# The last expert's second layer by token halves, with one of its two scatters moved ahead of a branch

## The chip, the cores and the metric

The kernel runs on one core of one Trainium2 chip. The metric is the device time of one execution in microseconds (us). Before the change the median of three executions was 429.29 us (428.25 to 430.55). One further execution was recorded by the hardware profiler and took 431.34 us.

Five engines run side by side, each with its own instruction sequence: TensorE (PE in the profile, with its weight loads as PEld), VectorE (DVE), ScalarE (ACT), GpSimd (POOL) and SyncE (SP). They meet only through semaphores. A suffix q (POOLq, ACTq) marks the sequencer of an engine: the part that reads instructions, waits for semaphores, loads registers and takes branches.

## The reference, cut to what matters

```python
attn_out = _attn_ref(q, k, v, s)                 # 2 x 8 heads, 576 rows, 64 wide
x = attn_out.transpose(0, 2, 1, 3).reshape(1152, 512)
x = _moe_ref(x, ...)                             # 8 experts, capacity 288
# second mixture: each token goes to one of 8 experts, 144 tokens each
for e in range(8):
    mask = assigned == e
    h = np.maximum(x[mask] @ w1[e], 0.0)         # 144 x 512 @ 512 x 1024
    out[mask] = h @ w2[e]                        # 144 x 1024 @ 1024 x 512
```

The change is in the last lines: the product `h @ w2[e]` of the eighth expert of the second mixture, and the way its 144 rows get to `out`.

## The kernel before, in words

The program is one long sequence: attention, routing, eight experts of the first mixture, routing, eight experts of the second mixture. Only the end matters here.

**One expert of the second mixture** (`moe2`, L2105) holds its 144 tokens as columns. The first layer (`layer1`, L992, matmuls on L1004 to L1006) makes `h`, 1024 by 144, in two 16-bit parts: a high part written by ACT (L1012) and a low part written by DVE (L1013). The second layer (`second2`, L2051) multiplies by `w2`. For the last expert `w2` too is held in two 16-bit parts; the low part is written by DVE on L164. So an output block of 128 features is 8 slices times 3 terms, 24 matmuls of 144 columns (L2059), in the order (high w, high h), (low w, high h), (high w, low h) for slice 0, then slice 1, and so on. Four blocks of features make 96 matmuls. Two blocks share a tile of PSUM, the accumulator memory, and ACT copies each finished pair to `y` (L2065).

**The rows go out** in two halves of 72 tokens (`turned2`, L2071; `out2`, L2084). PE turns a half of `y` by four transposes (L2075), an engine multiplies it with the gate weights (ACT on L2078, for the very last half DVE on L2080), and POOL issues an indirect DMA that scatters 72 rows of 512 numbers to `out` (L2085). For the experts before the last this happens during the next expert's work. For the last expert the two halves lie in the tiles named `XA` and `iotat`.

**The branch.** The routing checks itself (`checks`, L2021). All engines load a flag, `badi`, and skip a long repair block if it is zero (L2190, L2191):

```python
bv = nc.values_load(badi[0:1, 0:1], min_val=0, max_val=4 * E)
with tc.If(bv > 0):
    ...
last_rows()
```

The two last scatters are issued by `last_rows` (L2099), that is behind the branch, because the repair block writes the same rows. Their row numbers, `tokl` (L2045), point out of range when the check has failed, so that nothing is written then. A path that skips the block brings the semaphore counts to what the block would have made them (POOL: the instruction on L2191 called INC_SWDGE_SEM in the trace and ISA in the order of instructions).

**What sets the order.** Every engine works strictly through its own list, in the order in which the Python code emits instructions; a string of letters (`LAST`, L2165) places background steps at numbered points of an expert.

Of the kernel before, what the change touches and what calls it, by code (L numbers as in the profile page):

```python
# [9 lines left out]
F32 = mybir.dt.float32  # L10
# [3 lines left out]
AF = mybir.ActivationFunctionType  # L14
OP = mybir.AluOpType
# [6 lines left out]
def tile_attention_moe_moe(ctx: ExitStack, tc: tile.TileContext, q, k, v, s, wg1, w1a, w2a, capacity,  # L22
                           wg2, w1b, w2b, out, dbg=None):
    nc = tc.nc
    B, H, S, D = q.shape
    NTOK, DM = out.shape
    E = wg1.shape[1]
    FF = w1a.shape[2]
    CAP = int(capacity)
    P = 128  # L30
# [8 lines left out]
    CAP2 = NTOK // E  # L39
# [6 lines left out]
    C0, C1 = max(CAPS), min(CAPS) // 16 * 16  # L46
# [61 lines left out]
    given = set()  # L108
# [719 lines left out]
    for m in range(-7, NH + 3):  # L828
# [47 lines left out]
        for name in names:  # L876
            if m == NH - 1 and name == "X1":
                continue
            if name in tasks:
                tasks[name]()  # L880
                step0(m, name)
                if (m, name) in SCATTER0:
                    n = SCATTER0.index((m, name))
# [90 lines left out]
    def split_ws(i):  # L974
        def of(k, part):
            while (i + k, part) in split_queue and i >= 2 * E:
                pop_hi()
            while (i + k, part) in late:
                pop_lo()
            hi, lo = WS[i + k]  # L980
            return part_of((hi, lo), k, part)
        return of
# [9 lines left out]
    def layer1(p, ws, xt, N, after, tick=none, halved=8):  # L992

        h = p.get("h", hp).tile([P, 8, C0], F32, name="h")
        hh, hl = (x[:, :, :N] for x in h[:, :halved].rearrange("p c n -> p (c n)").bitcast(F16).rearrange(
            "p (k c n) -> k p c n", k=2, c=halved)) if halved else (None, None)
        h = h[:, :, :N]
        for fp in range(4):
            ph = p["ph"].tile([P, 2, N], F32)
            wh, wl = ws(0, fp)  # L1000
            for g in range(2):
                fs = slice(g * P, (g + 1) * P)
                for c in range(4):
                    nc.tensor.matmul(ph[:, g], wh[:, c, fs], xt[:, c], start=c == 0, stop=False)  # L1004
                    nc.tensor.matmul(ph[:, g], wh[:, c, fs], xt[:, 4 + c], start=False, stop=False)  # L1005
                    nc.tensor.matmul(ph[:, g], wl[:, c, fs], xt[:, c], start=False, stop=c == 3)  # L1006
                if g == 0:
                    tick(3 * fp)
            tick(3 * fp + 1)
            r = slice(2 * fp, 2 * fp + 2)  # L1010
            if 2 * fp < halved:
                nc.scalar.activation(hh[:, r], ph, AF.Relu)  # L1012
                nc.vector.scalar_tensor_tensor(hl[:, r], ph, 0.0, hh[:, r], op0=OP.max, op1=OP.subtract)  # L1013
            else:
                nc.scalar.activation(h[:, r], ph, AF.Relu)
            after(fp)
            tick(3 * fp + 2)
        return hh, hl, h
# [19 lines left out]
    def rows_of_w2(i, hs, halved):  # L1038

        w = loaded[i].rearrange("p (c f) -> p c f", c=8)  # L1040
        hh, hl, h = hs
        terms = [(w, h, f) for f in range(halved, 8)]
        if halved:
            while any(x[0] == i for x in split_queue):
                pop_hi()
            while any(x[0] == i for x in late):
                pop_lo()
            wh, wl = (x.rearrange("p (c f) -> p c f", f=DM) for x in WS[i])
            terms = [(a, b, f) for f in range(halved) for a, b in ((wh, hh), (wl, hh), (wh, hl))] + terms
        return terms  # L1050
# [65 lines left out]
    mo1, mo2 = {}, {}  # L1116
# [87 lines left out]
    S2 = CAP2 // 2  # L1204
# [200 lines left out]
    pend = None  # L1405
    for e in range(E):
# [14 lines left out]
        halved = 8 if e in HELD else 4 if e else 0  # L1421
        hs = layer1(mo1, split_ws(2 * e), XT1.pop((e, 0)), CAPS[e], after1, halved=halved)
# [7 lines left out]
        else:  # L1430
            ys = second1(mo1, 2 * e + 1, hs, halved, CAPS[e], after2)
            pend = (e, ys)
# [124 lines left out]
    gates = []  # L1557
# [157 lines left out]
    def pop_hi():  # L1715
        if split_queue:
            i, part = split_queue.pop(0)
            split_hi(i, part)
            late.append((i, part))

    def pop_lo():
        if late:
            split_lo(*late.pop(0))
# [94 lines left out]
    for t in range(NTT - 1):  # L1818
        nc.tensor.matmul(pp[:, t + 1:], ones, left[:, t:t + 1].to_broadcast([P, NTT - 1 - t]),
                         start=False, stop=t == NTT - 2, skip_group_check=True)  # L1820
# [17 lines left out]
    for t in range(NTT):  # L1838
        cm = gp.tile([P, CT, P], F16, name="g").rearrange("p t q -> p (t q)").bitcast(BF16)
        nc.vector.tensor_scalar(cm, iotac, pos[:, t:t + 1], None, op0=OP.is_equal)  # L1840
        for c in range(CT):
            nc.tensor.matmul(pL[:, c], cm[:, c * P:(c + 1) * P], S3[:, :, t], start=t == 0 and c == 0,
                             stop=t == NTT - 1 and c == CT - 1, skip_group_check=True)
# [10 lines left out]
    A = rp.tile([P, CN, E], F32, name="A")  # L1854
# [193 lines left out]
    tokl = rp.tile([S2, 2], I32, name="tokl")  # L2048
    pb2 = Banks("D1")

    def second2(i, hs, halved, tick):  # L2051
        terms = rows_of_w2(i, hs, halved)
        y = mo2["y"].tile([P, 4, C0], F32, name="y")[:, :, :CAP2]
        for dp in range(2):
            py = mo2["py"].tile([P, 2, CAP2], F32)
            for g in range(2):
                d = slice((2 * dp + g) * P, (2 * dp + g + 1) * P)
                for k, (a, b, f) in enumerate(terms):
                    nc.tensor.matmul(py[:, g], a[:, f, d], b[:, f], start=k == 0, stop=k == len(terms) - 1)  # L2059
                    if k == len(terms) - 5:  # L2060
                        tick(12 + 5 * dp + 2 * g)
                if g == 0:
                    tick(13 + 5 * dp)
            tick(15 + 5 * dp)
            nc.scalar.activation(y[:, 2 * dp:2 * dp + 2], py, AF.Copy)  # L2065
            if dp:
                given.add(i // 2)
            tick(16 + 5 * dp)
        return y

    def turned2(e, y, g2, q_, xo, banks, engine):  # L2071
        pb = banks.tile([P, 512], F32)[:S2].rearrange("p (c d) -> p c d", c=4)
        sl = slice(q_ * S2, (q_ + 1) * S2)
        for c in range(4):
            nc.tensor.transpose(pb[:, c], y[:, c, sl], identf)  # L2075
        pb = pb.rearrange("p c d -> p (c d)")
        if engine == "A":
            nc.scalar.activation(xo, pb, AF.Copy, scale=g2[:, q_:q_ + 1])  # L2078
        else:
            nc.vector.tensor_scalar(xo, pb, g2[:, q_:q_ + 1], None, op0=OP.mult)  # L2080

    scattered = []

    def out2(rows, xo):  # L2084
        i = nc.gpsimd.indirect_dma_start(  # L2085
            out=out[:, :], out_offset=bass.IndirectOffsetOnAxis(ap=rows, axis=0),
            in_=xo, in_offset=None, bounds_check=NTOK - 1, oob_is_err=False)
        for o in scattered:
            tc.declare_no_dep(i.ins, o.ins, reason="distinct rows")
        scattered.append(i)  # L2090

    def back2(e, y, g2, q_):
        xo = mo2["o"].tile([SL, DM + E + 1], F32, name="x2f")[:S2, :DM]
        turned2(e, y, g2, q_, xo, pb2, "A")
        out2(tok[:, e, q_:q_ + 1], xo)

    xl = [x[:S2].bitcast(F32)[:, :DM] for x in (XA.rearrange("p c n -> p (c n)"), iotat)]

    def last_rows():  # L2099

        scattered.clear()
        for h in range(2):
            out2(tokl[:, h:h + 1], xl[h])

    def moe2(script, first=False):  # L2105
        pend = None
        given.difference_update(range(E, 2 * E))
        for e in range(E):
            i0 = 2 * E + 2 * e

            def tick(k, e=e):
                if first and (e, k) == (E - 1, 0):
                    nc.gpsimd.drain()
                for c in script(e, k):
                    if c == "h":
                        pop_hi()
                    elif c == "l":
                        pop_lo()
                    elif c in "01":
                        if pend is not None:  # L2120
                            back2(*pend, int(c))
                            if first and (e, c) == (E - 2, "0"):
                                nc.gpsimd.drain()
                    elif c == "w":
                        next(work, None)
                    elif e + 1 < E:
                        XT1[e + 1] = spread(xg[e + 1], XT1.get(e + 1), "st".index(c))
                        if c == "t":
                            del xg[e + 1]
                    load_next()  # L2130
                    gather_next()

            halved = HALVED2[e]
            hs = layer1(mo2, split_ws(i0), XT1.pop(e), CAP2, none, tick, halved)
            pend = (e, second2(i0 + 1, hs, halved, tick), gates[0])
            gates.pop(0)
        pbl = Banks("D1 A1")
        for q_ in range(2):
            if first:
                turned2(*pend, q_, xl[q_], pbl, "AD"[q_])  # L2140
            else:
                back2(*pend, q_)

    def steps():
        yield from phases()
# [16 lines left out]
    THEN = "w h l h l0 w w . . . w 1l h wl h l wh l s tl wh l"  # L2162
    FLOAT = "w . . . 0 w w . . . w 1l h wl h l wh l s tl wh l"
    MORE = "w h l h l0 wh wl . . . w 1l h wl h l wh l s tl wh l"
    LAST = "w h l h l0 wh wl h l . w 1 . w . . w . . . w ."  # L2165
    AGAIN = [x.split() for x in [{0: FLOAT, 4: THEN, 6: MORE}[n] for n in HALVED2[:-1]] + [LAST]]
    SCRIPTS = [FIRST.split(), SECOND.split()] + AGAIN[2:]
    next(work)
# [80 lines left out]
```

## Time and profile before

| | |
|---|---|
| median of three executions | 429.29 us |
| profiled execution | 431.34 us |
| its span in the trace | 429.5 us |
| rest around the span | 1.84 us |
| PE busy | 394.1 us (92%) |
| DVE, ACT, POOL busy | 334.3, 258.5, 192.4 us |
| span from the last expert's transposes (421.64) to the end | 7.9 us |

The span is counted from the first instruction to the last. Busy times include the pipeline's depth, and those of different engines overlap. A line of the timeline gives start, duration, engine, source line, operation and tiles; x19 means that 19 instructions were merged into the line. A sequencer's row gives how often an instruction ran, its shortest, median and longest duration in ns, and the first and last start.

### The profile page before, as it was taken

To read this page: it belongs to the slowest core of one execution; us is meant where nothing else is said; L and a number is where in the kernel's file an instruction comes from. 1 tells how busy PE (TensorE), PEld (TensorE's weight loads), DVE (VectorE), ACT (ScalarE), POOL (GpSimd) and SP (SyncE) were. 2 spreads that over 40 slices of the span, in tenths; PEclk is the share of its full clock that TensorE was granted. 3 is DMA by queue.
4 is the path that set the end of the run, shared out by engine and by line. 5 is a ranking of instruction groups with operands and counts; after the bars stand their busy time and mean duration, and the time that the engine had idled before them with its cause. 6 is when DMAs were issued, how large, how long until landed. Compare 5 with 4: busy or idle time off the path is not lost.

```text
span 429.5 us, 14026 instructions
## 1 busy us (share of the span) xinstructions
PE 394.1 (92%) x5408; PEld 364.3 (85%) x5408; DVE 334.3 (78%) x969; ACT 258.5 (60%) x466; POOL 192.4 (45%) x310
## 2 busy tenths in 40 slices
PE   1669999998889999999999999988999999989993
PEld 1448888887768899999999998946999999989993
DVE  7879999989684566777688796688587887988860
ACT  4448888886564165564665681716365766867761
POOL 4378788885781433052141364641243333333021
PEclk9988999999957999999999999966999999999998
DMA  7798898985847669999999976159989999998811
GB/s 138 170 223 191 198 206 217 218 207 168 303 166 186 238 188 363 301 287 365 347 334 332 344 133 111 28 150 319 339 269 346 334 311 323 281 331 289 260 44 34
DMA packets 91327, 103.04 MB, mean 240 GB/s; under 512 B 56136, under 2 KB 59208, under 8 KB 91251
## 3 DMA queue, kind: packets, MB, share of 16 engines
q1 hardware_dynamic: 85859, 91.85, 74.0%
q0 software_dynamic: 4192, 9.91, 7.6%
q8 instruction: 44, 0.72, 0.7%
q10 hardware_dynamic: 1200, 0.30, 0.3%
q14 instruction: 32, 0.26, 0.2%
HBM read 81.42 MB, written 14.59 MB: 224 GB/s over the span
## 4 chain that ended last, share of the span: by engine, by line
PE 66%; DVE 15%; DMA 11%; issue 4%; ACT 2%; SPq 1%; POOL 1%; POOLq 0%; DVEq 0%; ACTq 0%
PE C L1061 12%; DMA xg<-x2d,tok 6%; PE C L2059 4%; PE A L1004 4%; PE A L1006 4%; PE A L1005 4%; PE pog L559 4%; DVE wl L164 4%; PE pT L452 4%; PE pM L476 2%; PE A L2059 2%; DMA cb<-cumd 2%; PE pE L528 2%; PE pE L529 2%; PE D L2059 2%
## 5 line engine op out<-in xcount | busy, mean ns | idle before, releaser
L164 DVE TENSOR_TENSOR wl<-wf,wh 128x1024 bf16<-128x1024 f32 x64 | 78.1, 1242 | 21.6 <-ACT wh L160 21.0
L160 ACT ACTIVATE wh<-wf 128x1024 f16<-128x1024 f32 x64 | 65.6, 1049 | 15.1 <-DMA wf<-in_moe_w_dram 15.1
L1004 PE MATMUL A<-xt,wh 128*128 128x144 f16 (+4 forms) x288 | 59.6, 232 | 0.0
L1006 PE MATMUL A<-xt,wl 128*128 128x144 f16 (+4 forms) x288 | 59.6, 231 | 0.0
L1005 PE MATMUL A<-xt,wh 128*128 128x144 f16 (+4 forms) x288 | 59.6, 231 | 0.0
L1061 PE MATMUL C<-h,wf 128*128 128x160 f32 (+7 forms) x544 | 58.5, 269 | 0.0
L1006 PEld LDWEIGHTS <-wl 128*128 128x128 bf16 x512 | 50.4, 99 | 1.8 <-issue 1.8
L1176 POOL DMA_INDIRECT x2d<-xo,tix x14 | 24.3, 1732 | 61.2 <-DVE l L1193 23.7
L1004 PEld LDWEIGHTS <-wh 128*128 128x128 f16 x512 | 50.5, 99 | 0.7 <-issue 0.5
L1005 PEld LDWEIGHTS <-wh 128*128 128x128 f16 x512 | 50.4, 99 | 0.7 <-issue 0.3
L164 DVE TENSOR_TENSOR wf<-wf,wf 128x1024 bf16<-128x1024 f32 x33 | 39.5, 1219 | 3.4 <-ACT wf L160 3.4
L414 POOL TENSOR_TENSOR pl<-pf,ph 128x512 f16<-128x512 f32 x30 | 35.7, 1202 | 10.0 <-DVE ph L403 7.9
L536 ACT ACTIVATE pf<-pE,XB 128x512 f32<-128x512 f32 (+4 forms) x80 | 36.5, 509 | 4.9 <-PE pE L531 4.5
L1551 POOL DMA_INDIRECT xg<-x2d,tok x16 | 20.0, 1251 | 42.3 <-PE A L2059 10.2
L1061 PEld LDWEIGHTS C<-h,wf 128*128 128x128 f32 x256 | 36.2, 190 | 0.1
L488 DVE CUSTOM_DVE_ANT_0 junk<-pM,cb 128x128 f16<-128x128 f32 (+4 forms) x80 | 32.0, 430 | 4.4 <-PE pM L478 2.7
L160 ACT ACTIVATE wf<-wf 128x1024 f16<-128x1024 f32 x33 | 34.4, 1051 | 0.0
L476 PE MATMUL pM<-al,ar 128*128 128x128 f16 (+2 forms) x96 | 26.9, 320 | 7.2 <-DVE rm L488 7.0
L2085 POOL DMA_INDIRECT out_dram<-x2f,tok x14 | 17.1, 1220 | 35.1 <-ACT h L1012 17.7
L2059 PE MATMUL C<-h,wf 128*128 128x144 f16 (+1 forms) x324 | 31.9, 251 | 0.4 <-DVE wf L164 0.3
L559 PE MATMUL pog<-vf,pf 128*128 128x65 f32 x180 | 30.7, 296 | 0.0
L2059 PEld LDWEIGHTS <-wf 128*128 128x128 f16 (+1 forms) x408 | 26.2, 98 | 1.1 <-issue 0.5
(455 smaller groups left out, 1181.6 us busy)
## 6 DMA issues: line engine op xcount, KB each, us to landing
wf<-in_moe_w_dram SPq DMA_DIRECT2D x128, 512.0 KB, 7.9
xd<-zero SPq DMA_DIRECT2D x18, 257.0 KB, 4.7
cb<-cumd SPq DMA_DIRECT2D x16, 288.0 KB, 5.3
x2d<-zero SPq DMA_DIRECT2D x9, 260.5 KB, 5.6
kf<-in_k_dram SPq DMA_DIRECT2D x16, 128.0 KB, 4.0
vf<-in_v_dram SPq DMA_DIRECT2D x16, 128.0 KB, 3.4
qf<-in_q_dram SPq DMA_DIRECT2D x14, 128.0 KB, 4.2
bl<-al SPq DMA_DIRECT2D x16, 72.0 KB, 4.9
```

Source lines behind the costliest of these rows:

```text
L160: nc.scalar.activation(hi, src, AF.Copy)
L164: nc.vector.tensor_sub(lo, src, hi)
L414: (nc.gpsimd if ENG[name][i % 2] == "P" else nc.vector).tensor_sub(o, x, y)
L476: nc.tensor.matmul(o, AR[m][:, t * P:(t + 1) * P], AL[m][:, j0:j1], start=True, stop=not diag)
L488: nc.vector.tensor_tensor_reduce(junk[:w, :j1 - j0], o, CB[m][:w, j0:j1], 1.0, r if t == 4 and j0 == 0 else -3e38, OP.add, OP.max, r)
L536: nc.scalar.activation(d, o, AF.Exp, bias=x, scale=2.0 ** -13)
L559: nc.tensor.matmul(o, pf[:, c:c + P], VF[n % 4][:, j, h], start=False, stop=j == t)
L1004: nc.tensor.matmul(ph[:, g], wh[:, c, fs], xt[:, c], start=c == 0, stop=False)
L1005: nc.tensor.matmul(ph[:, g], wh[:, c, fs], xt[:, 4 + c], start=False, stop=False)
L1006: nc.tensor.matmul(ph[:, g], wl[:, c, fs], xt[:, c], start=False, stop=c == 3)
L1061: nc.tensor.matmul(py[:, g], a[:, f, d], b[:, f], start=k == 0, stop=k == len(terms) - 1)
L2059: nc.tensor.matmul(py[:, g], a[:, f, d], b[:, f], start=k == 0, stop=k == len(terms) - 1)
```

## The change

The second layer of the last expert, in the first pass only, is done by the new function `last2`: first all four blocks of features for tokens 0 to 71, then all four for tokens 72 to 143. That makes 192 matmuls of 72 columns where 96 of 144 stood, and four copies by ACT where there were two. The transposes, the scaling and the scatter of the first half stand behind the first two blocks of the second half, so that the scatter of `XA` is emitted ahead of the branch. The second half (`iotat`) is turned at the end, its columns 0 to 255 are scaled by DVE and 256 to 511 by ACT, and it alone is scattered behind the branch. The letters of `LAST` are moved to the new numbering of points.

```diff
@@ turned2 @@
-        if engine == "A":
-            nc.scalar.activation(xo, pb, AF.Copy, scale=g2[:, q_:q_ + 1])
-        else:
-            nc.vector.tensor_scalar(xo, pb, g2[:, q_:q_ + 1], None, op0=OP.mult)
+        n = DM // len(engine)
+        for k, x in enumerate(engine):
+            o, i = (a[:, k * n:(k + 1) * n] for a in (xo, pb))
+            if x == "A":
+                nc.scalar.activation(o, i, AF.Copy, scale=g2[:, q_:q_ + 1])
+            else:
+                nc.vector.tensor_scalar(o, i, g2[:, q_:q_ + 1], None, op0=OP.mult)
@@ last_rows @@
-        scattered.clear()
-        for h in range(2):
-            out2(tokl[:, h:h + 1], xl[h])
+        scattered[:] = ahead_of_it
+        out2(tokl[:, 1:], xl[1])
+
+    ahead_of_it = []
+
+    def last2(e, i, hs, halved, tick):
+        terms = rows_of_w2(i, hs, halved)
+        y = mo2["y"].tile([P, 4, C0], F32, name="y")[:, :, :CAP2]
+        pbl = Banks("D1 A1")
+        k = 12
+        for q_ in range(2):
+            sl = slice(q_ * S2, (q_ + 1) * S2)
+            for dp in range(2):
+                py = mo2["py"].tile([P, 2, S2], F32)
+                for g in range(2):
+                    d = slice((2 * dp + g) * P, (2 * dp + g + 1) * P)
+                    for j, (a, b, f) in enumerate(terms):
+                        nc.tensor.matmul(py[:, g], a[:, f, d], b[:, f, sl], start=j == 0, stop=j == len(terms) - 1)
+                    tick(k)
+                    k += 1
+                nc.scalar.activation(y[:, 2 * dp:2 * dp + 2, sl], py, AF.Copy)
+                if q_ == 0:
+                    tick(k)
+                    k += 1
+                if (q_, dp) == (1, 0):
+                    turned2(e, y, gates[0], 0, xl[0], pbl, "A")
+                    ahead_of_it.append(out2(tokl[:, :1], xl[0]))
+        given.add(i // 2)
+        turned2(e, y, gates[0], 1, xl[1], pbl, "DA")
@@ moe2 @@
-            pend = (e, second2(i0 + 1, hs, halved, tick), gates[0])
+            if first and e == E - 1:
+                last2(e, i0 + 1, hs, halved, tick)
+            else:
+                pend = (e, second2(i0 + 1, hs, halved, tick), gates[0])
             gates.pop(0)
-        pbl = Banks("D1 A1")
-        for q_ in range(2):
-            if first:
-                turned2(*pend, q_, xl[q_], pbl, "AD"[q_])
-            else:
-                back2(*pend, q_)
+        for q_ in range(0 if first else 2):
+            back2(*pend, q_)
@@ the script of the last expert @@
-    LAST = "w h l h l0 wh wl h l . w 1 . w . . w . . . w ."
+    LAST = "w h l h l0 wh wl h l . w 1 w . w . w . w . w ."
```

POOL's list just ahead of the branch, before the change (`x2f` is the scaled half of the seventh expert; the names in brackets are the semaphores that an instruction waits for, DMASW those of POOL's own DMAs):

```order
L2085 DMA out_dram<-x2f,tok 1152x512 [waits DMASW2_49,Activation_49]
L2085 DMA out_dram<-x2f,tok 1152x512 [waits DMASW3_49,Activation_49]
L2085 DMA out_dram<-x2f,tok 1152x512 [waits DMASW4_49,Activation_49]
L2190 TENSOR_LOAD badi [waits DMAHW2_49,DMAHW3_49,DMAHW1_49,DMAHW5_49,DMAHW0_49,DMAHW7_49,DVE_49,PE_49]
L2191 COMPARE_AND_BRANCH
```

The same place after the change:

```order
L2088 DMA out_dram<-x2f,tok 1152x512 [waits DMASW3_49,Activation_49]
L2088 DMA out_dram<-x2f,tok 1152x512 [waits DMASW4_49,Activation_49]
L2088 DMA out_dram<-XA,tokl 1152x512 [waits DMASW5_49,Activation_49]
L2219 TENSOR_LOAD badi [waits DMAHW2_49,DMAHW3_49,DMAHW1_49,DMAHW5_49,DMAHW0_49,DMAHW7_49,DVE_49,PE_49]
L2220 COMPARE_AND_BRANCH
```

The scatter of `XA` has moved in front of the load of the flag, and the load and the branch now stand behind it in POOL's list.

POOL's list where the skipping path joins again, before the change (ISA is the instruction that sets the counts; two branches around it enclose the skipping path):

```order
L2191 UNCONDITIONAL_BRANCH
L2191 ISA [waits Pool_49,Pool_sequencer_49,DMASW4_49,DMASW5_49,DMASW3_49,DMASW6_49,DMASW2_49,DMASW7_49,DMASW1_49,DMASW0_49]
L2191 UNCONDITIONAL_BRANCH
L2085 DMA out_dram<-XA,tokl 1152x512 [waits DMASW3_49,DMASW4_49,DMASW2_49,DMASW5_49,DMASW1_49,DMASW6_49,DMASW0_49,Activation_49]
L2085 DMA out_dram<-iotat,tokl 1152x512 [waits DMASW6_49,DVE_49]
```

The same place after the change:

```order
L2088 DMA out_dram<-x2f,tok 1152x512 [waits DMASW5_49,Activation_49]
L2220 UNCONDITIONAL_BRANCH
L2220 ISA [waits Pool_49,Pool_sequencer_49,DMASW4_49,DMASW5_49,DMASW3_49,DMASW6_49,DMASW2_49,DMASW7_49,DMASW1_49,DMASW0_49]
L2220 UNCONDITIONAL_BRANCH
L2088 DMA out_dram<-iotat,tokl 1152x512 [waits DMASW4_49,DMASW3_49,DMASW5_49,DMASW2_49,DMASW6_49,DMASW1_49,Activation_49]
```

One scatter is left behind the join, and it now waits for ACT.

ACT's list at the end, after the change (before it, the rows were two copies to `y` of 128x2x144, then `XA` of 72x512, then the load of the flag):

```order
L2125 ACTIVATE y<-C_8322 128x2x72 [waits PE_49]
L2125 ACTIVATE y<-A_8372 128x2x72 [waits PE_49]
L2125 ACTIVATE y<-D_8422 128x2x72 [waits PE_49]
L2081 ACTIVATE XA<-D_8472,gq 72x512 [waits DVE_49,PE_49]
L2125 ACTIVATE y<-C_8481 128x2x72 [waits PE_49]
L2081 ACTIVATE iotat<-A_8531,gq 72x256 [waits DVE_49]
L2219 TENSOR_LOAD badi [waits DMAHW2_49,DMAHW3_49,DMAHW1_49,DMAHW5_49,DMAHW0_49,DMAHW7_49,DVE_49,PE_49]
```

Scaling `XA` now stands between the third and the fourth copy, and ACT's share of `iotat`, which reads what PE's last transposes wrote, waits for DVE.

## Rows read from the trace of the kernel before

**Rows 1.** The profile's page: span, and PE's busy time.

```profile
span 429.5 us, 14026 instructions
PE 394.1 (92%) x5408; PEld 364.3 (85%) x5408; DVE 334.3 (78%) x969; ACT 258.5 (60%) x466; POOL 192.4 (45%) x310
```

**Rows 2.** The timeline from 412.6 us to the end.

```profile
414.44 0.60 PE L2075 MATMUL D<-identf,y 128*72 128x128 f32 x4
...
414.87 1.35 PE L2059 MATMUL C<-h,wf 128*128 128x144 f16 x19
...
415.12 0.68 ACT L2078 ACTIVATE x2f<-D,gq 72x512 f32<-72x512 f32 x1
...
416.10 1.18 POOL L2085 DMA_INDIRECT out_dram<-x2f,tok  x1 [2.28 <-ACT x2f L2078]
416.39 0.45 DVE L1013 SCALAR_TENSOR_TENSOR h<-C,h 128x288 f16<-128x288 f32 x1
...
416.53 2.27 PE L2059 MATMUL C<-h,wf 128*128 128x144 f16 x29 [0.31 <-DVE wf L164]
...
418.64 3.16 PE L2059 MATMUL A<-h,wf 128*128 128x144 f16 x48
...
421.84 0.41 ACT L2065 ACTIVATE y<-A 128x288 f32<-128x288 f32 x1 [2.59 <-PE A L2059]
...
422.31 0.41 PE L2075 MATMUL D<-identf,y 128*72 128x128 f32 x2 [0.28 <-ACT y L2065]
...
422.75 0.68 ACT L2078 ACTIVATE XA<-D,gq 72x512 f32<-72x512 f32 x1 [0.50 <-PE D L2075]
423.19 0.75 DVE L2080 TENSOR_SCALAR iotat<-A,gq 72x512 f32<-72x512 f32 x1 [6.35 <-PE A L2075]
423.73 0.93 POOL L2085 DMA_INDIRECT out_dram<-XA,tokl  x1 [6.45 <-ACT XA L2078]
424.97 0.93 POOL L2085 DMA_INDIRECT out_dram<-iotat,tokl  x1 [0.30 <-issue]
```

**Rows 3.** The instructions of line L2190, the load of the flag, on POOL.

```profile
L2190 POOLq EVENT_SEMAPHORE  x4: 17/42/43, 415.8 to 416.1; - x4
...
L2190 POOLq TENSOR_LOAD <-badi x1: 502/502/502, 416.2 to 416.2; - x1
```

**Rows 4.** The instructions of line L2191, the branch, on POOL and DVE.

```profile
L2191 POOLq EVENT_SEMAPHORE  x6: 17/30/43, 419.4 to 419.8; - x6
...
L2191 DVEq EVENT_SEMAPHORE  x2: 21/21/21, 427.5 to 427.6; - x2
...
L2191 POOLq COMPARE_BRANCH  x1: 58/58/58, 416.7 to 416.7; - x1
L2191 POOLq INC_SWDGE_SEM  x1: 240/240/240, 419.9 to 419.9; - x1
...
L2191 DVEq COMPARE_BRANCH  x1: 72/72/72, 424.2 to 424.2; - x1
```

**Rows 5.** The chain that ended last, from 416 us: start, duration, what.

```profile
420.54 2.94 issue
...
423.73 0.93 POOL out_dram L2085
```

**Rows 6.** PE's timeline in an earlier stage, matmuls of 68 columns.

```profile
268.78 1.28 PE L1329 MATMUL C<-h,wf 128*128 128x68 f16 x36
...
272.56 2.76 PE L1329 MATMUL C<-h,wf 128*128 128x68 f16 x84
```

**Rows 7.** DMA issues from 423 us: KB, median us from issue to landing.

```profile
out_dram<-XA,tokl POOLq DMA_INDIRECT x1, 3.5
out_dram<-iotat,tokl POOLq DMA_INDIRECT x1, 3.0
```

**Rows 8.** DMA issues from 415.9 to 416.5 us.

```profile
out_dram<-x2f,tok POOLq DMA_INDIRECT x1, 3.1
```

**Rows 9.** Line L2085, all sixteen scatters.

```profile
DMA to landing us min/median/max: 2.8/4.8/7.7
```

More of the change, by code (lines that the diff above doesn't have):

```diff
@@ L2090, in out2 @@
         scattered.append(i)
+        return i
     def back2(e, y, g2, q_):
```

## The prediction

> **What bounds the kernel now.** I read the page first: PE is busy for 92% of a 429.5 us span [rows 1], so until the end of the last expert PE sets the pace. Then I read the timeline of the end, because the change touches nothing before 414.87 us. The reader is to see three stretches there [rows 2]. PE works on the second layer from 414.87 us. The last copy to `y` starts at 421.84, and transposes, scaling and two scatters follow in single file: `XA` is scaled from 422.75 to 423.43, its scatter starts at 423.73, the scatter of `iotat` at 424.97. Nothing computes after that: the last scatter lands 3.0 us after its start [rows 7], at 427.97, and the span ends 1.53 us later. So each microsecond by which the last scatter starts later is one microsecond of time, and the whole question is when that scatter can start. The chain of waits [rows 5] names POOL as the engine that the end hangs on, and says that POOL stood ready from 420.54 and waited 2.94 us for `XA`. Last I read what POOL's sequencer did before 420.54 [rows 3, 4], because the change puts new work ahead of that.
>
> **Part 1: the matmuls by halves.** It removes 96 matmuls of 144 columns and adds 192 of 72. The pace of the old ones comes from two merged lines: 3.16 us for 48 and 1.35 us for 19 [rows 2], a difference of 1.81 us for 29, or 62.4 ns each. For 72 columns there is a close relative earlier in the trace, 68 columns with a fresh weight load each: 2.76 us for 84 and 1.28 us for 36 [rows 6], or 30.8 ns each. The line through both gives 0.416 ns per column and 32.5 ns for 72 columns. The total grows from 5.99 to 6.24 us.
>
> More is lost at the start. PE gets through 19 matmuls and is held there [rows 2]: the 20th needs the low part of w2 and the 21st the low part of h, which DVE finishes at 416.84. Counting back from 418.64, where the 49th starts, the 21st started at 418.64 - 28 x 0.0624 = 416.89. The hold stays, since DVE's list is the same up to there, but only 20 half-size matmuls are behind it instead of 20 full ones. Left are 171 steps of 32.5 ns = 5.56 us instead of 75 of 62.4 = 4.68 us: 0.88 us later. The four transposes of the first half, moved between the blocks, take another 0.43 us of PE (414.44 to 414.87 [rows 2]).
>
> **Part 2: when the first half is ready.** Its transposes stand behind the 144th matmul, 123 steps after the 21st: 416.89 + 4.00 = 420.89. They start at about 420.95 and last 0.60, ACT starts 0.08 later (415.04 to 415.12 in the earlier instance) and needs 0.68 [rows 2]: `XA` is scaled at 422.31. The copy that stands before it on ACT has been done by then: PE finished its input near 421.1, and a copy of twice its width took 0.41 [rows 2]. The scatter starts 0.30 after scaling, as in both instances (415.80 to 416.10, 423.43 to 423.73 [rows 2]): 422.61, or 1.12 us earlier than before.
>
> **Part 3: what POOL must do between the two scatters.** This is the wait that the change adds. Behind the first scatter on POOL's list now stand the load of the flag, the branch and the join, and the second scatter queues behind them. The trace before shows that very sequence once, behind the scatter of `x2f`: scaled at 415.80; load 416.2 to 416.7 [rows 3]; branch at 416.7; then nothing until the first instruction of the join at 419.4; six semaphore instructions, INC_SWDGE_SEM from 419.9 to 420.14 [rows 4]; the preparation of the next scatter, ready at 420.54 [rows 5]. From "scaled" to "ready" that is 4.74 us. Before, 2.94 us of waiting followed, so it cost nothing: the cover was PE's own second layer. Now the first half is scaled only at 422.31, so POOL is ready at 427.05, and the scatter starts 0.25 later (423.48 to 423.73 [rows 5]): 427.30.
>
> The empty 2.64 us after the branch is the price in doubt. Two things can fill it, and both come again: the jump over the repair block, and the landing of the scatter just issued, for which the join waits by the order of instructions (`x2f`: 3.1 us [rows 8], 416.10 + 3.1 = 419.2). The Trainium skill, page "Runtime: NRT & Kernel Launch", section "Instruction fetch mechanics", states that "Branching breaks sequential prefetch": a taken branch to a target outside the loaded window stalls until it is fetched. The rows agree in kind, and by that rule the sum above stands whatever becomes of the landing; the page gives no price. From below, the gap could cost nothing: then POOL needs 0.96 + 1.14 = 2.10 us, is ready at 424.41, and the data decide. From above, DVE's gap after the same branch was 427.5 - 424.27 = 3.23 us [rows 4], 0.6 us more, and `XA` landed after 3.5 us [rows 7], 0.4 more than `x2f`. I take 2.64, the row of the same engine in the same place.
>
> **Part 4: when the second half is ready.** 421.40 + 47 steps = 422.93 for its last matmul, some 0.25 to the copy, 0.25 for a copy of half the width, 0.06 and 0.41 for the last two transposes [rows 2]: 423.9. DVE needs some 0.4 us for half of what took 0.75 [rows 2]. ACT's half waits for DVE, so the two engines go one after the other: done near 424.8, scatter possible at 425.1. That is 2.2 us before POOL is ready, so the split of the scaling buys nothing, and its being serial costs nothing.
>
> **The sum.** The last scatter moves from 424.97 to 427.30: +2.33 us. Landing and the end stay (3.0 + 1.53): span 431.83. With the 1.84 us around the span the profiled execution would take 433.67 against 431.34. The median of the runs shown lies 2.05 us below that execution, so I add the difference to the median: 429.29 + 2.33 = 431.6 us. By bounds: +0.1 (no gap), +2.9 (DVE's gap), +3.1 with a slower landing on top.
>
> **Rivals.**
>
> *The join is passed in the shadow of the second half.* The gap shrinks to nothing or near it, because the target is at hand or the landing was all that filled it and comes early. For it speaks that the first scatter starts 1.12 us earlier; against it that the same engine showed 2.64 us behind the same kind of scatter. It decides if the passage takes under 2.5 us from "scaled" instead of 4.74. Then the scatter starts at 425.1, +0.1 us: 429.4, not slower. Chance 0.15.
>
> *The join waits for a slow landing.* The sixteen scatters landed after 2.8 to 7.7 us, with a median of 4.8 [rows 9]. With 4.8, `XA` lands at 427.41, 1.5 us after the join would begin: +3.8 us, 433.1. Against it: the three last scatters, with no weights being loaded, took 3.0 to 3.5 [rows 7, 8]. Chance 0.08.
>
> *Narrow matmuls keep the pace of wide ones,* since each still loads 128 columns of weights. With 62.4 ns instead of 32.5, 123 steps end 3.7 us later and the last scatter starts 6.0 us later than before: 435.3. The 84 matmuls of 68 columns [rows 6] speak against it. The Trainium skill, page "TensorE: Matmul & The Clock Gate", section "LDWEIGHTS (loading the stationary operand)", puts a load at columns / 1.2 ns, 107 ns for 128; by that rule alone the 123 steps would end 9.2 us later, and the trace's 30.8 ns for a load and a matmul together disagrees. Chance 0.04.
>
> **How the numbers follow.** The forecast has 0.68, with its own range from 431.0 to 432.6; the rest, 0.05, is for what I don't see. A change of 0.5%, 2.15 us, is about what a measurement of this kernel can tell from none. The forecast lies only just beyond that, and the three runs spread over 2.3 us; I count about two thirds of it as slower. With the slow landing and the slow matmuls that makes 0.56 slower. The other third of the forecast, the first rival and part of the rest make 0.37 the same. No step here saves 2.15 us, so faster has 0.07. The range from 429.4 to 433.0 leaves out half of the first rival and of the second, and the third.
>
> **What would show it.** Right: PE's 72-column matmuls at 32 to 33 ns; `XA` scaled near 422.3 after the same start; POOL's branch near 423.3, its join from 425.9, and the second scatter near 427.3, with ACT's half of `iotat` scaled over 2 us earlier; that scatter released by POOL itself in the chain. Wrong: the second scatter within 0.4 us of its data, a join that begins under 2 us after the branch, or matmuls above 40 ns.

## The result, and the profile after

The changed kernel is slower: its median is 433.99 us (431.66 to 435.45, 6 executions) against 428.71 us before (427.9 to 430.55, 6 executions), a ratio of 1.012 with a 95% interval of 1.0086 to 1.0154. The forecast was slower, 431.6 us; the time lies outside its range (429.4 to 433.0), and the slowdown of 1.2% is more than twice the 0.54% of the forecast. A ratio with its interval is estimated over the executions of both kernels without the slow ones (over 1.5% above the fastest of the same kernel), and need not equal the quotient of the two medians.

The profiled executions do not show this at first sight: 431.34 us before, 431.66 after, spans of 429.5 and 429.9. The two differ in an earlier stage, which the change doesn't touch. These are the rows of the windows view for 120 to 150 us, before and then after: window, its length, busy time of PE, PEld, DVE, ACT and POOL with counts, granted clock, DMA share, GB/s.

```profile
120.00:150.00 30.00, 28.03 (x318) 24.28 (x316) 18.64 (x60) 11.05 (x22) 13.13 (x13) 0.77 0.59 182
```

```profile
120.00:150.00 30.00, 26.48 (x361) 23.12 (x360) 19.72 (x60) 14.13 (x27) 15.75 (x27) 1.00 0.64 214
```

PE was granted 0.77 of its clock there in the execution before, so it spent part of the 30 us at 1.2 instead of 2.4 GHz, and was behind from then on: the same DVE instructions run 0.6 us later than after the change at 113 us, 4.5 later at 141, and, as some of it comes back between 240 and 300 us, 3.4 later from 314 us to the last layer. Comparing ends of spans would therefore hide the change. I compare from a common point: the *release*, the end of DVE's last L1013, for which PE is held in the second layer. Before it lies at 416.39 + 0.45 = 416.84 [rows 2], after at 413.47. From there to the end of the span it took 12.66 us before and 16.43 after: **3.77 us more**, 0.88%, which lies just inside the measured interval.

The timeline of the tail after (two stretches of it):

```profile
413.02 0.45 DVE L1013 SCALAR_TENSOR_TENSOR h<-C,h 128x288 f16<-128x288 f32 x1
413.16 0.21 PE L2122 MATMUL C<-h,wf 128*128 128x72 f16 x1 [0.81 <-DVE wf L164]
...
414.43 1.73 PE L2122 MATMUL A<-h,wf 128*128 128x72 f16 x48
...
417.55 0.61 PE L2075 MATMUL D<-identf,y 128*72 128x128 f32 x4
...
418.19 0.68 ACT L2081 ACTIVATE XA<-D,gq 72x512 f32<-72x512 f32 x1 [0.15 <-PE D L2075]
419.17 0.93 POOL L2088 DMA_INDIRECT out_dram<-XA,tokl  x1 [5.26 <-ACT XA L2081]
...
420.55 0.48 DVE L2083 TENSOR_SCALAR iotat<-A,gq 72x256 f32<-72x256 f32 x1 [7.08 <-PE A L2075]
421.06 0.47 ACT L2081 ACTIVATE iotat<-A,gq 72x256 f32<-72x256 f32 x1 [1.02 <-DVE iotat L2083]
424.71 0.94 POOL L2088 DMA_INDIRECT out_dram<-iotat,tokl  x1 [4.61 <-issue]
```

The reader is to see the gap between the last two lines. The second half is scaled at 421.53, and its scatter starts at 424.71: over 3 us in which no data is missing. ACT's half also starts only when DVE's has ended (released by DVE, 421.06).

What POOL's sequencer does in that time, first the load of the flag, then the branch and the join (in [rows 3, 4] the same lines before):

```profile
L2219 POOLq EVENT_SEMAPHORE  x4: 17/42/43, 418.9 to 419.2; - x4
...
L2219 POOLq TENSOR_LOAD <-badi x1: 505/505/505, 419.2 to 419.2; - x1
```

```profile
L2220 POOLq EVENT_SEMAPHORE  x6: 17/30/43, 422.8 to 423.2; - x6
...
L2220 POOLq COMPARE_BRANCH  x1: 58/58/58, 419.8 to 419.8; - x1
L2220 PEldq COMPARE_BRANCH  x1: 3716/3716/3716, 421.4 to 421.4; - x1
...
L2220 POOLq INC_SWDGE_SEM  x1: 260/260/260, 423.3 to 423.3; - x1
```

The branch is at 419.8, the join begins at 422.8. The end of the chain of waits (start, duration, what):

```profile
423.88 0.59 issue
424.47 1.18 POOLq L2273
```

In [rows 5] the line at this place was a wait of 2.94 us for `XA`. Now POOL is ready at 423.88 with everything it waits for done, and still needs 0.59 us to issue. The landings from 420 us, before [rows 7]:

```profile
out_dram<-XA,tokl POOLq DMA_INDIRECT x1, 3.3
```

```profile
out_dram<-iotat,tokl POOLq DMA_INDIRECT x1, 3.6
```

### The profile page after: what moved, and what is told of

The parts are those of the page before. It is cut to its first block, busy times and chain, and to the rows that moved or that the text cites. A ratio compares the mean times of both kernels' runs of the same rounds, so it can differ in the third digit from the quotient of the medians.

```text
span 429.9 us, 14220 instructions
## 1 busy us (share of the span) xinstructions
PE 389.1 (91%) x5504; PEld 360.3 (84%) x5504; DVE 333.5 (78%) x969; ACT 258.8 (60%) x469; POOL 192.6 (45%) x310
## 4 chain that ended last, share of the span: by engine, by line
PE 62%; DVE 16%; DMA 13%; issue 4%; ACT 2%; SPq 1%; POOL 0%; POOLq 0%; DVEq 0%; ACTq 0%
PE C L1061 12%; DMA xg<-x2d,tok 10%; PE A L1004 4%; PE A L1006 4%; PE A L1005 4%; PE C L2059 4%; DVE wl L164 4%; PE pT L452 3%; PE pog L559 3%; PE pM L476 3%; PE A L2059 2%; PE pE L528 2%; PE pE L529 2%; DVE wf L164 2%; DMA wf<-in_moe_w_dram 2%
## 5 line engine op out<-in xcount | busy, mean ns | idle before, releaser
L1006 PE MATMUL A<-xt,wl 128*128 128x144 f16 (+4 forms) x288 | 60.7, 234 | 0.0
L1005 PE MATMUL A<-xt,wh 128*128 128x144 f16 (+4 forms) x288 | 60.6, 234 | 0.0
L1004 PE MATMUL A<-xt,wh 128*128 128x144 f16 (+4 forms) x288 | 60.6, 234 | 0.0
L559 PE MATMUL pog<-vf,pf 128*128 128x65 f32 x180 | 28.7, 282 | 0.0
L2059 PE MATMUL C<-h,wf 128*128 128x144 f16 (+1 forms) x276 | 28.4, 255 | 0.0
L1005 PE MATMUL C<-xt,wh 128*128 128x144 f16 x128 | 24.7, 226 | 1.4 <-DVE xt L1576 1.4
```

Source lines behind the costliest of these rows:

```text
L559: nc.tensor.matmul(o, pf[:, c:c + P], VF[n % 4][:, j, h], start=False, stop=j == t)
```

## The experiments

All counts below are in us from the release, each taken from that kernel's own timeline; the tail runs from the release to the end of the span.

| kernel | start of XA's scatter | start of the last scatter | it lands after | tail |
|---|---|---|---|---|
| before | 6.89 | 8.13 | 3.0 | 12.66 |
| changed | 5.70 | 11.24 | 3.6 | 16.43 |
| c1, changed again | 5.70 | 11.16 | 4.5 | 17.27 |
| e1, both behind | 5.71 | 8.36 | 3.5 | 13.52 |
| e2, copy ahead | 10.99 | 12.24 | 3.0 | 16.76 |
| e3, short block with scatters | 5.70 | 10.24 | 2.8 | 14.55 |
| e4, short block without DMA | 5.69 | 9.12 | 2.8 | 13.44 |
| e5, full width, scatter ahead | 6.89 | 12.82 | 2.8 | 17.15 |
| e6, halves with filled wait | 5.08 | 8.27 | 3.4 | 13.14 |
| e7, full width with filled wait | 6.12 | 7.36 | 2.8 | 11.72 |

**c1: the changed kernel again**, without an edit.

> The changed kernel once more, for its tail and its time. Both theories count from the release of the hold, the end of DVE's last L1013 (before: 416.84, after: 413.47); the tail from there to the end of the span was 12.66 us before and 16.43 us after. Theory (POOL's join between the two scatters costs 3.8 us, the rest of the measured difference comes from how the earlier stages fell in the runs): tail 16.2 to 16.7 us again, and a time that moves with the clock granted between 120 and 150 us. Rival (the change slows the stages before the tail as well): the tail is the same, but the release comes later than 416.8 us in an execution whose clock is full throughout.

Measured: 432.38 us (430.44 to 434.67, 12 executions) against 428.29 (23 executions), ratio 1.0083, interval 1.0054 to 1.0112. Tail 17.27, above the expected 16.7: the last scatter started at the same place (11.16), but landed after 4.5 us.

```profile
out_dram<-iotat,tokl POOLq DMA_INDIRECT x1, 4.5
```

The release came at 413.03, earlier than in both executions above. No traced execution has a full clock throughout, so the rival's own test can't be made; but outside the stretches in which the granted clocks differ, DVE's instructions keep a steady distance to those of the kernel before (4.2 to 4.3 us from 141 to 250 us, 3.8 from 314 us on), so nothing there shows slower stages ahead of the tail. Whether the time of the other executions moves with the clock between 120 and 150 us was not looked at: one execution of each kernel is traced. The first sample's 1.2% and this one's 0.8% are both in keeping with a tail longer by 3.8 to 4.6 us.

**e1: both scatters behind the branch again**, all else as changed.

```diff
     def last_rows():
-        scattered[:] = ahead_of_it
-        out2(tokl[:, 1:], xl[1])
+        scattered.clear()
+        for h in range(2):
+            out2(tokl[:, h:h + 1], xl[h])
...
                     turned2(e, y, gates[0], 0, xl[0], pbl, "A")
-                    ahead_of_it.append(out2(tokl[:, :1], xl[0]))
```

> Halves and split scaling as changed, but both scatters behind the branch again. Theory (the branch on POOL is the whole loss): XA's scatter starts 5.7 us after the release, iotat's 8.4, tail 12.9 us, 0.2 above before; time within 0.3% of before. Rival (192 narrow matmuls, four copies and a serial scaling are the loss): tail above 14.5 us, at least 0.5% slower than before.

Measured: ratio 1.0014, interval 0.9979 to 1.005 (12 executions). Its two scatters in the timeline, and the POOL lines of the branch:

```profile
420.79 0.93 POOL L2088 DMA_INDIRECT out_dram<-XA,tokl  x1 [5.26 <-ACT XA L2081]
...
423.44 0.94 POOL L2088 DMA_INDIRECT out_dram<-iotat,tokl  x1 [1.72 <-ACT iotat L2081]
```

```profile
L2220 POOLq EVENT_SEMAPHORE  x6: 17/30/43, 417.8 to 418.2; - x6
...
L2220 POOLq COMPARE_BRANCH  x1: 58/58/58, 415.0 to 415.0; - x1
```

The scatters start 5.71 and 8.36 us after the release, as expected, and each is released by its data (ACT). The branch and the join are done by 418.6, in the shadow of PE. So the halves, the extra copies and the serial scaling cost 0.23 us at the last scatter (8.36 against 8.13); the other 2.88 us by which it starts later in the changed kernel go with the place of one scatter. The tail is 0.6 above the expected 12.9 chiefly because the last scatter landed after 3.5 instead of 3.0 us.

**e2: a copy in the scatter's place.** It separates the jump from the landing.

```diff
-                    ahead_of_it.append(out2(tokl[:, :1], xl[0]))
+                    nc.gpsimd.tensor_copy(mark, xl[0][:, :1])
```

with both scatters behind the branch as in e1.

> As e1, but POOL copies one column of XA where the changed kernel has the scatter, so that load, branch and join stand behind the first half without a DMA in flight. Theory A (the jump over the repair block fills the gap after the branch): the first instruction of the join comes 2.6 to 3.0 us after the branch, XA's scatter starts 11.2 us after the release and iotat's 12.4, tail 17.0 us. Theory B (the landing of the scatter fills it): the join begins within 0.5 us of the branch, scatters at 8.5 and 9.7, tail 14.3 us.

Measured (one execution): theory A. The branch is at 421.8, the join begins at 424.4:

```profile
L2222 POOLq EVENT_SEMAPHORE  x6: 17/30/43, 424.4 to 424.9; - x6
...
L2222 POOLq COMPARE_BRANCH  x1: 58/58/58, 421.8 to 421.8; - x1
```

The latest scatter of POOL before it (`x2f`) had started at 414.69, 7 us before the branch. So 2.6 us pass with no scatter left to land (one like it took 3.1 us [rows 8]): the jump alone fills the gap. Scatters at 10.99 and 12.24, tail 16.76, as expected to 0.3 us.

**e3: a short repair block that still has scatters.**

```diff
     with tc.If(bv > 0):
-        with tc.If(nc.values_load(overi[0:1, E:E + 1], min_val=0, max_val=1) > 0):
-            overflown()
-        route_all()
...
-        moe2(again)
+        scattered.clear()
+        for e in range(E):
+            out2(tok[:, e, :1], xl[0])
```

> The changed kernel with a repair block of eight scatters only (the repair itself is left out; it does not run with these inputs), so that the branch has a near target while the join still waits for all of POOL's DMAs. Theory A (jump): the join is no longer late by a jump; what is left is the landing of XA, 3.3 us after its start, so the last scatter starts 9.8 to 10.6 us after the release instead of 11.24: tail 15.0 to 15.8. Theory B (landing alone): nothing changes, tail 16.4. If neither a jump nor a landing holds the join here, the data decide: 8.4 and a tail near 13.

Measured (one execution): theory A's first bound.

```profile
L2220 POOLq EVENT_SEMAPHORE  x4: 17/42/43, 420.0 to 422.1; - x4
...
L2220 POOLq COMPARE_BRANCH  x1: 50/50/50, 419.8 to 419.8; - x1
L2220 PEldq COMPARE_BRANCH  x1: 228/228/228, 421.4 to 421.4; - x1
...
L2220 POOLq INC_SWDGE_SEM  x1: 260/260/260, 422.2 to 422.2; - x1
```

The join now begins 0.2 us after the branch (420.0), and PE's branch takes 228 ns instead of 3716. But its last semaphore instruction stands at 422.1: `XA`, started at 419.15, landed 2.8 us later, at 421.95. So each of the two can hold POOL by itself, and they run side by side: the jump until 422.8 in the changed kernel, where `XA` had landed at 422.5, and the landing until about 422.1 here. Last scatter at 10.24, inside the expected 9.8 to 10.6.

**e4: neither.**

```diff
     with tc.If(bv > 0):
...
+        nc.vector.tensor_copy(badf[:, :1], badf[:, :1])
```

> The changed kernel with a repair block of one tiny VectorE operation (the repair is left out; it does not run with these inputs): a near target, and no DMA of POOL in the block, so that the join waits for no landing. Theory (jump and landing each held the join: 2.6 us with no DMA in flight in e2, some 2.2 us with no jump in e3): with both gone the data decide, the last scatter starts 8.4 us after the release instead of 11.24, lands after 2.8 to 3.0 us, tail 12.7 to 13.0. Rival (something else in the passage holds POOL, such as the load of the flag or the checks of the semaphores): last scatter at 9.5 or later, tail above 13.8.

Measured (one execution): POOL is ready 0.5 us after the branch (423.6) and then waits for data.

```profile
424.07 2.06 issue
426.13 1.19 POOLq L2253
```

The scatter started at 9.12 and not at 8.4, because ACT began the last copy to `y` 0.77 us later than in the changed kernel (1.65 us after its previous work instead of 0.88):

```profile
424.31 0.29 ACT L2125 ACTIVATE y<-C 128x144 f32<-128x144 f32 x1 [1.65 <-PE C L2122]
```

So the expectation for the start failed by that, while what it was to tell came out: with jump and landing gone, POOL no longer decides. Why ACT was late here (and in e6) I did not find; both ran on another chip than c1, e1, e2 and e3, where it was on time, and no run tells whether that matters.

**e5: the scatter alone moved, full width.**

```diff
     def last_rows():
 
-        scattered.clear()
-        for h in range(2):
-            out2(tokl[:, h:h + 1], xl[h])
+        scattered[:] = ahead_of_it
+        out2(tokl[:, 1:], xl[1])
...
                 turned2(*pend, q_, xl[q_], pbl, "AD"[q_])
+                if q_ == 0:
+                    ahead_of_it.append(out2(tokl[:, :1], xl[0]))
```

> The kernel before, full-width second layer, with nothing changed but the scatter of XA, which stands ahead of the branch. XA is scaled 6.6 us after the release, 1.2 later than with halves. Theory (passage of 5.0 us and 0.83 to the start): last scatter 12.4 us after the release, tail 17.0 to 17.8 against 12.66: 1.0 to 1.2% slower than before, more than with halves. Rival (the halves are what costs): tail at most 14, within 0.4% of before.

Measured: ratio 1.0128, interval 1.0072 to 1.0184 (4 executions); last scatter at 12.82, tail 17.15. Its data were there from 423.75, and POOL started it at 429.47:

```profile
429.47 0.94 POOL L2085 DMA_INDIRECT out_dram<-iotat,tokl  x1 [5.01 <-issue]
```

The theory holds, though the last scatter started 0.4 us later than it said, and the rival (the halves are what costs) falls from the other side.

**e6 and e7: filling PE's wait.** In the changed kernel and in the one before, PE waits ahead of the 20th matmul [rows 2]. Both versions let it do 19 matmuls of the next PSUM tile first; e7 in the kernel before, e6 with the halves of e1 and the second half scaled by DVE alone.

Of e7's edit (`part` emits one matmul; `halved == 8` holds for the last expert):

```diff
+        n = 19 if halved == 8 else 0
         for dp in range(2):
-            py = mo2["py"].tile([P, 2, CAP2], F32)
+            for k in range(n):
+                part(dp, 0, k)
+        for dp in range(2):
             for g in range(2):
-                d = slice((2 * dp + g) * P, (2 * dp + g + 1) * P)
-                for k, (a, b, f) in enumerate(terms):
-                    nc.tensor.matmul(py[:, g], a[:, f, d], b[:, f], start=k == 0, stop=k == len(terms) - 1)
+                for k in range(0 if g else n, len(terms)):
+                    part(dp, g, k)
```

> A version that might beat both: halves, both scatters behind the branch as in e1, the second half scaled by DVE alone, and in the first half the first 19 matmuls of one block of each of the two PSUM tiles stand ahead of the 20th, so that 38 run while PE would wait for DVE. Theory: PE gains 19 x 32.6 = 0.62 us and DVE alone is 0.25 us quicker than the two in turn, so the last scatter starts 7.5 us after the release (e1: 8.36) and the tail is 12.0 to 12.6, 0.1 to 0.6 us shorter than before: not to be told from before by time. Rival (the order of the matmuls costs PE): tail above 13.

> The kernel before with the same filling of the wait at full width in the last expert: 19 matmuls of the second PSUM tile stand ahead of the 20th of the first. Theory: the 0.8 us for which PE waited (416.1 to 416.9) is filled, both scatters move 0.8 us ahead, tail 11.8 to 12.0 us against 12.66, 0.2% faster. Rival (the copy of the first tile now comes too late, or POOL's join at 3.7 us after the release holds XA): tail 12.6 or more.

Measured for e7: the last scatter at 7.36 instead of 8.13, tail 11.72; by time the same as before (ratio 1.0003, interval 0.9974 to 1.0032, 12 executions). Measured for e6: ratio 0.9986, interval 0.9958 to 1.0015; XA's scatter moved ahead by 0.63 us (5.08), as expected, but the last scatter stayed at 8.27 and the tail is 13.14, a miss. The tail is where the rival had it, but not by the rival's mechanism: PE's last 48 matmuls start 3.91 us after the release (e1: 4.53), so the new order gained time on PE. ACT's last copy came late as in e4, and the last scatter landed after 3.4 us:

```profile
422.19 0.29 ACT L2137 ACTIVATE y<-C 128x144 f32<-128x144 f32 x1 [1.64 <-PE C L2126]
```

PE's idle time can be filled, and at full width that is worth 0.77 us at the start of the last scatter. No version here beats the kernel before by more than a measurement can tell.

## Why the prediction was wrong in size

The direction and the mechanism came out; what failed is the size of the sum, above all in part 3. It put the end 2.33 us later, the traced tail is 3.77 us longer, and the medians differ by 5.28. The step from 2.33 to 3.77 is accounted for below; the one from there to 5.28 is only argued.

**Part 1, the pace of narrow matmuls: right.** The 48 of the second PSUM tile start at 414.43, those of the third at 415.99: 1.56 / 48 = 32.5 ns, as predicted.

**Part 2, when `XA` is scaled: right.** 418.87 is 5.40 us after the release; predicted 422.31 - 416.84 = 5.47. The scatter followed 0.30 later.

**Part 3, the mechanism: right, its price too low.** POOL's passage decides; e1, e2 and e5 show it by taking it away, by putting it there without a landing, and by putting it there without the halves. Three terms of the sum were too small:

- *Passage from "scaled" to "ready"*: 423.88 - 418.87 = 5.01 us instead of 4.74. The jump took some 0.3 us longer than at [rows 4]; over the runs it took 2.6 us (e2) to 3.3 (e5), so the row of before was at the short end.
- *From "ready" to the start of the scatter*: 0.83 us instead of 0.25. This term was read from the wrong kind of row. The 0.25 came from a scatter that POOL had already taken up and that only waited for `XA` [rows 5]. The first scatter behind the join, with its wait over when POOL reaches it, takes the sequencer another 0.59 us ahead of that 0.25: 0.59 in the changed kernel, 0.57 to 0.59 in c1, e2, e3 and e5. Before, the 2.94 us of waiting hid it. It does not show either where a scatter queues right behind another: `iotat` before was scaled at 423.94 and started at 424.97, 0.31 us after the scatter of `XA` ended.
- *Landing and end*: 5.19 us from the start to the end of the span instead of 4.53, most of it the landing (3.6 instead of 3.0). The first two terms come back in c1 (start at 11.16); this one is scatter, since landings of this same scatter took 2.8 to 4.5 us over the runs.

Together 0.27 + 0.58 + 0.66 = 1.51, less 0.07 from part 2: 1.44, which is 3.77 - 2.33. Of the bounds, the +3.1 "with a slower landing on top" does not follow from its terms either: 2.33 + 0.6 + 0.4 is 3.3.

**Part 4: right, and idle.** The second half was scaled at 8.06 (predicted 424.8 - 416.84 = 8.0), DVE and ACT in turn.

**The doubt about the gap: the jump, with the landing close behind it.** I let jump and landing stand as two readings of one gap. e2 and e3 show that each can hold POOL by itself. In the changed kernel the jump ended last (422.8; `XA` landed at 419.17 + 3.3 = 422.5), as it did before (419.4 against 419.2). The Trainium skill, page "Runtime: NRT & Kernel Launch", section "Instruction fetch mechanics", says that a taken branch out of the loaded window stalls for a fetch; the traces agree, 2.6 us with nothing to land (e2) and 0.2 with a near target (e3). The DMA view has a trace of such a fetch as well: in each of the eight traces with the long block a packet of kind instruction, 8 KB on queue q14, starts 1.0 us after POOL's branch (before at 417.7, changed at 420.8, e2 at 422.8), and between branch and last scatter there is none in e3 and e4. The view does not say whose packet it is; that it is POOL's is read from its place in time.

**The rivals.** *In the shadow of the second half*: no, the passage was 5.0 us where under 2.5 was needed. *Slow landing at the join*: not at the join, since `XA` landed after 3.3 us, before the join began. *Narrow matmuls at the pace of wide ones*: no. A load of weights does last 0.10 us by its own row (PEld at L2122, 95 to 100 ns), but one load and one matmul pass every 32.5 ns, so the loads overlap, and what one lasts is not what it costs.

**The rest of the distance.** 3.77 us on 428.71 make 432.5, inside the range; the median of six was 433.99, and that of the twelve in c1 lies 4.1 us above another sample of the kernel before (3.6 by the ratio). I take the remaining 1.5 us of the first sample for scatter over executions, which span 3.8 us there. That is argued from the two samples and not shown; the tail of the unprofiled executions isn't known.

## What to carry to other kernels

Work moved ahead of a branch makes its engine take the branch later, and whatever the engine still has to do behind the branch pays for the jump. So first look where each engine's branch lies in time and what hides it: here POOL took the branch during PE's last layer for nothing, and the move put it between the last two scatters. And a duration read from an instruction that was waiting is only what was left after the wait; what it costs from a standing start has to be read from one that did not wait.

## What I had not expected of the hardware

- The landing of an identical scatter of 72 rows varied from 2.8 us (e3, e4, e5, e7) to 3.4 to 3.6 (e1, e6, changed) and 4.5 (c1). Those without a jump of another engine under way (e2, e3, e4, e5) took 2.8 to 3.0, but e7 took 2.8 with jumps under way, and before it was 3.0 with them; what decides stays open.
- Skipping the full block costs every engine, not POOL alone: PE's branch took 3.5 to 4.3 us over it, and 0.23 over the short ones. How the cost grows between the two lengths was not measured.
- ACT's last copy started 0.77 us late in e4 and e6 with its input ready, and on time in the other kernels with halves. Not explained.
